# A gated linear-attention layer feeding a two-layer network: the values of a wide step multiplied behind the next step's scores and states, and a new plan for the front

## The chip, the cores and the metric

The kernel runs on one core of one Trainium2 chip. The metric is the time of one execution on the device in microseconds (us), lower is better. Times are medians of several executions; the profile shows one execution.

## The reference

For each of 4 batches and 8 heads a recurrence runs over 768 positions with head dimension 40. It keeps a 40x40 matrix `C` and a vector `n`, decayed by a forget gate and fed by an input gate (both stabilised by a running maximum `m`). The output is gated, and the gated rows of all heads (320 wide, 3072 tokens) go through two matrix products with a softplus between:

```python
C = f_stab * C + i_stab * einsum('bhd,bhe->bhde', v_t, k_t)
n = f_stab * n + i_stab * k_t
denom = maximum(abs(n . q_t), 1.0)
y_t = sigmoid(o_t) * (C q_t) / denom
out = softplus(y @ w_in) @ w_out        # 320 -> 2048 -> 320
```

## The kernel before, in words

**Tiling.** The 3072 tokens are cut into 24 chunks of 128 tokens (one batch, 128 positions); a *step* `s` computes the attention of one chunk, all 8 heads. Three steps make a *tile* of 384 tokens; there are 8 tiles `t`. For each tile and each of 16 column blocks `f` of the hidden layer, `products()` issues 8 matmuls 128x128 by 384 into a PSUM tile `hp` (line 931; operands are split in a high and a low part, hence 8), ScalarE takes softplus twice (lines 819, 820), VectorE forms the low part `gl` (line 823), and 9 matmuls 128x128 by 320 add into the three output tiles `po` (line 894). A block's 9 output matmuls come two blocks after its `hp`. So TensorE's stream is: 8 of `hp`, 9 of `po`, 8 of `hp`, and so on, 128 blocks in all.

**Steps.** Steps 0 to 5 are *plain*; they must be ready before or soon after the products begin. Steps 6 to 23 (tiles 2 to 7) are *wide*. A wide step has: `load`, `fb` (decays from DRAM), `scan` (line 403), `vw` and `vi` (values weighted for the states and for the outputs, line 417), `ga` = `scores` (line 444, 32 trace records of small matmuls), `st` = `states` (line 457, 32 records), `pm` (`by_decays`, line 465, VectorE reads the scores), `cp` (`keep_states`, ScalarE copies the states out), `old`, `mid`, `new` (the recurrent state on GpSimd), `gc` = `values_wide` (lines 606 and 618, 32 records each), `ym`, `ya` (lines 625, 629: VectorE reads the values), `yd`, `rd` (a round trip through DRAM that turns the layout), `fin`, `end`, `xh`, `xl` (normalise, gate, split; the slice of `X` that the tile's products read).

**What sets the order.** `products()` counts its own large matmuls, `n` = 17 a block. Each piece of other work is an event with a due value of `n`; `tick(n)` issues all events that are due behind the n-th large matmul, and each engine then runs its instructions in that order. Due values come from offsets in `wide_step` (line 804) relative to a `base` per step, and, for steps 0 to 8, for the weight conversions and for the gates, from the table `WHEN` (line 988). `PICK` (line 1038) names engines (V VectorE, A ScalarE, G GpSimd), `WARM` how many filler matmuls `keep_warm` (line 697) issues at each of 11 places in the front. `CHAIN` and `needed` (lines 735, 743) only assert that the order is legal.

**PSUM.** Of eight banks `ps_h` has three, one bank each (tag `hp`), `ps_a` one pair (tag `pa`), the outputs three. Before, a wide step's scores and states share the pair, and the same step's values take the pair some 20 `n` later:

```python
z.ga = pair(f"ga{z.n}", spare)                    # line 437
z.gc = gc = pair(f"gc{z.n}")                      # line 597
("ga", scores, 14), ("st", states, 14), ... ("gc", values_wide, 36),
```

Of the kernel before, what the change touches and what calls it, by code (L numbers as in the profile page):

```python
# [40 lines left out]
def mlstm_moe_kernel(  # L41
# [393 lines left out]
    def scores(z, spare=False):  # L435

        z.ga = pair(f"ga{z.n}", spare)
        for i in range(2):
            for q in range(NQ):
                ts = slice(q * Q, (q + 1) * Q)  # L440
                for y in range(2):
                    for x in range(2):
                        rows, g = slice(x * PP, x * PP + D), y * 2 + i
                        nc.tensor.matmul(  # L444
                            z.ga[y * Q : (y + 1) * Q, x, (i * NQ + q) * Q : (i * NQ + q + 1) * Q],
                            z.k[rows, g, ts], z.q[rows, g, ts], start=True, stop=True,
                        )
        z.qs = range(1 if z.last else NQ)

    def states(z):  # L450

        for q in z.qs:
            for i in range(2):
                for y in range(2):
                    for x in range(2):
                        j, w, c0 = (q * 2 + i) * 2 + x, D if x else PP, CP0 + (q * 2 + i) * E
                        nc.tensor.matmul(  # L457
                            z.ga[x * PP : x * PP + w, y, c0 : c0 + E],
# [4 lines left out]
    def by_decays(z):  # L463
        pw = z.pw.rearrange("p (x z) t -> p x (z t)", x=2)
        nc.vector.tensor_tensor(pw, z.ga[:, :, 0:CP0], pw, op=ALU.mult)  # L465
        z.pm = z.pw

    def keep_states(z):
        z.cp = p2.tile([PP + D, 2, NQ, 2, E], F32, tag="cp", bufs=4, name=f"cp{z.n}")
        w = len(z.qs) * 2 * E  # L470
        copy(
            pick(f"cp{z.id}", "A"),
            z.cp[:, :, 0 : len(z.qs)].rearrange("p y q z e -> p y (q z e)"), z.ga[0 : PP + D, :, CP0 : CP0 + w]
# [269 lines left out]
    def needed(kind, z):  # L743
        need = [(k, z.s) for k in CHAIN.get(kind, "").split()]
        if kind == "xh":
            need.append(("end" if z.wide else "xp", z.s))
        if kind in ("mid", "new", "gc") and z.c > 0:
# [43 lines left out]
    def plain_step(z, times):  # L791
# [3 lines left out]
            ga=lambda z: scores(z, z.s in SPARE_A), pm=by_decays, st=states, cp=keep_states, old=decay_old,  # L795
# [8 lines left out]
    def wide_step(z, base):  # L804
        d = 18 + 30 * (z.s == NH)
        for name, f, t in (
            ("fb", decays, -64), ("load", load, -48), ("vi", gate_values, -12), ("scan", decay, -8), ("vw", state_values, 2),
            ("old", decay_old, 6), ("fc", load_decays, 8), ("ga", scores, 14), ("st", states, 14), ("pm", by_decays, 19),
            ("cp", keep_states, 21), ("mid", mid_state, 24), ("new", new_state, 30), ("gc", values_wide, 36),
            ("ym", scale_wide, 42), ("ya", add_wide, 42), ("yd", write_wide, 45), ("rd", read_wide, 78),  # L810
            ("fin", finish_wide, 127 + d), ("end", end_wide, 128 + d), ("xh", high_wide, 131 + d), ("xl", low_wide, 134 + d),
# [173 lines left out]
    def finished(t):  # L985
        return all(s in ended for s in range(t * NG, (t + 1) * NG))

    WHEN = {'l0': -300, 'p0': -299, 'k0': -298, 'wl0': -297, 'p1': -296, 'j0': -295, 'load0': -294, 'w0_0_0': -293,
# [155 lines left out]
```

## Time and profile before

| | |
|---|---|
| median of 3 runs | 454.08 us (452.62 to 455.22) |
| the profiled execution | 449.44 us |
| its span, first to last instruction | 447.3 us |
| TensorE busy | 430.3 us (96%) |
| VectorE, ScalarE, GpSimd busy | 265.7, 212.2, 93.4 us |
| mean granted TensorE clock | 0.992 of full speed |

How to read it: a row of the timeline has a start, a duration and an instruction group with its count; successive matmuls overlap in the pipeline, so the pace is the distance between starts, not the duration. Records of small fp32 matmuls are twice the matmuls in the code.

### The profile page before, as it was taken

The page shows a single profiled execution, that of the slowest core. Times are in us where ns is not written, and L with a number is a line of the kernel's source. Part 1 is how long each engine was busy: PE and PEld are TensorE (multiplying, and loading weights), DVE is VectorE, ACT ScalarE, POOL GpSimd, SP SyncE. Part 2 cuts the span into 40 slices and gives each one's busy share as a digit, 9 for nine tenths or more (in the row PEclk, how much of TensorE's full clock was granted, in tenths as well). Part 3 has the DMA queues.
Part 4 walks back from the last instruction along what each step waited for, and adds up shares of the span by engine and source line. Part 5 has one row for each costly group of instructions (what it writes and reads, how often), then busy time and mean ns, then how long its engine had stood idle before and what let it go on. Part 6 is the DMA issues. An engine that isn't in the chain of part 4 may idle for free.

```text
span 447.3 us, 12745 instructions
## 1 busy us (share of the span) xinstructions
PE 430.3 (96%) x5312; PEld 410.7 (92%) x5312; DVE 265.7 (59%) x469; ACT 212.2 (47%) x458; POOL 93.4 (21%) x158
## 2 busy tenths in 40 slices
PE   6788899999999999999999999999999999999996
PEld 6668788998999999999999999999999999999996
DVE  5897999778878565456456465465465465322211
ACT  4678885668436323544236333453236333333332
POOL 1621343523222311311311311111211210000000
PEclk9969999999999999999999999999999999999999
DMA  7788597752654542643353443644443530001001
GB/s 200 217 252 256 159 246 194 252 150 93 165 129 147 164 135 78 164 118 105 113 146 88 128 122 86 168 92 121 123 119 107 135 92 24 20 1 44 1 0 45
DMA packets 52089, 55.93 MB, mean 125 GB/s; under 512 B 5664, under 2 KB 42176, under 8 KB 52032
## 3 DMA queue, kind: packets, MB, share of 16 engines
q1 hardware_dynamic: 49008, 51.68, 41.3%
q10 hardware_dynamic: 3024, 3.44, 2.2%
q8 instruction: 41, 0.67, 0.6%
q14 instruction: 16, 0.13, 0.1%
HBM read 46.47 MB, written 8.64 MB: 123 GB/s over the span
## 4 chain that ended last, share of the span: by engine, by line
PE 84%; DVE 6%; DMA 5%; ACT 2%; issue 1%; SPq 1%; ACTq 0%; DVEq 0%
PE hp L931 38%; PE po L894 37%; DMA wr<-in_w_in 3%; PE ga L444 3%; PE gc L606 2%; PE gc L618 2%; PE ga L457 2%; DMA qk<-in_qk 1%; DMA fz_d<-g 1%; DVE wil L296 1%; DVE sgi L258 1%; DVE wol L306 1%; DVE sgo L258 1%; DVE pw L465 1%; SPq L277 0%
## 5 line engine op out<-in xcount | busy, mean ns | idle before, releaser
L931 PE MATMUL hp<-X,wih 128*128 128x384 f32 x768 | 180.7, 340 | 0.0
L819 ACT ACTIVATE gh<-hp 128x384 fp32r<-128x384 f32 x128 | 62.9, 491 | 175.0 <-PE hp L931 160.4
L931 PEld LDWEIGHTS hp<-X,wih 128*128 128x128 f32 x768 | 132.7, 188 | 1.6 <-DVE X L685 0.3
L823 DVE TENSOR_TENSOR gl<-hp,gh 128x384 fp32r<-128x384 f32 x128 | 70.7, 555 | 99.1 <-ACT hp L820 98.9
L894 PE MATMUL po<-wol,gh 128*128 128x320 f32 x384 | 81.9, 312 | 0.0
L894 PE MATMUL po<-woh,gh 128*128 128x320 f32 x384 | 81.3, 311 | 0.0
L894 PE MATMUL po<-woh,gl 128*128 128x320 f32 x384 | 80.6, 310 | 0.7 <-DVE gl L823 0.7
L931 PE MATMUL hp<-X,wil 128*128 128x384 f32 x256 | 66.2, 338 | 0.0
L894 PEld LDWEIGHTS po<-woh,gh 128*128 128x128 f32 x384 | 65.1, 188 | 0.7 <-issue 0.3
L894 PEld LDWEIGHTS po<-woh,gl 128*128 128x128 f32 x384 | 62.3, 188 | 1.2 <-DVE gl L823 1.0
L894 PEld LDWEIGHTS po<-wol,gh 128*128 128x128 f32 x384 | 62.8, 188 | 0.6 <-issue 0.2
L820 ACT ACTIVATE hp<-hp 128x384 f32<-128x384 f32 x128 | 62.2, 486 | 0.0
L931 PEld LDWEIGHTS hp<-X,wil 128*128 128x128 f32 x256 | 46.2, 188 | 0.2
L417 POOL TENSOR_TENSOR vw<-vt,gw 128x328 f32<-128x328 f32 x21 | 16.2, 770 | 108.7 <-DVE gw L408 100.6
L403 DVE TENSOR_TENSOR_SCAN pw<-fb,ident 128x512 f32<-128x512 f32 x24 | 29.1, 1212 | 0.0
L465 DVE TENSOR_TENSOR pw<-ga,pw 128x512 f32<-128x512 f32 x23 | 15.8, 686 | 18.0 <-PE ga L457 17.6
L515 POOL TENSOR_TENSOR c<-c,cp 104x164 f32<-104x164 f32 x20 | 10.1, 506 | 75.7 <-ACT cp L728 70.0
L625 DVE TENSOR_TENSOR y<-gc,y 112x512 f32<-112x512 f32 x18 | 12.4, 691 | 19.0 <-PE gc L618 19.0
L444 PEld LDWEIGHTS ga<-qk 40*64 40x64 f32 x736 | 13.0, 134 | 6.6 <-issue 4.4
L728 ACT COPY cp<-ga 104x328 f32<-104x328 f32 (+1 forms) x22 | 9.2, 416 | 19.3 <-DVE pw L465 15.0
L417 POOL TENSOR_TENSOR values_in<-vt,gT 128x328 f32<-128x328 f32 x16 | 12.1, 756 | 28.2 <-PE gc L618 18.8
L444 PE MATMUL ga<-qk 40*64 40x64 f32 x736 | 16.3, 224 | 1.4 <-DMA qk<-in_qk 0.9
(153 smaller groups left out, 434.7 us busy)
## 6 DMA issues: line engine op xcount, KB each, us to landing
vt<-in_vk SPq DMA_DIRECT2D x24, 324.0 KB
qk<-in_qk SPq DMA_DIRECT2D x48, 160.0 KB
fb<-fz_d SPq DMA_DIRECT2D x42, 128.0 KB
wo<-in_w_out SPq DMA_DIRECT2D x8, 640.0 KB
wr<-in_w_in SPq DMA_DIRECT2D x8, 512.0 KB
eg<-in_oT SPq DMA_DIRECT2D x6, 576.0 KB
yd<-y SPq DMA_DIRECT2D x36, 96.0 KB
out<-ob ACTq DMA_DIRECT2D x21, 160.0 KB
```

Source lines behind the costliest of these rows:

```text
L403: nc.vector.tensor_tensor_scan(z.pw.rearrange(flat), z.fb.rearrange(flat), ident4.rearrange(flat), 0.0, ALU.mult, ALU.add)
L417: e.tensor_tensor(to, of, by.unsqueeze(3).broadcast_to([to.shape[0], a, b, w]), op=ALU.mult)
L444: nc.tensor.matmul(z.ga[y * Q : (y + 1) * Q, x, (i * NQ + q) * Q : (i * NQ + q + 1) * Q], z.k[rows, g, ts], z.q[rows, g, ts], start=True, ...
L465: nc.vector.tensor_tensor(pw, z.ga[:, :, 0:CP0], pw, op=ALU.mult)
L515: nc.gpsimd.tensor_tensor(heads(z.cm), heads(z.cm), z.cp[:, :, 0], op=ALU.add)
L625: nc.vector.tensor_tensor(y2, z.gc[0 : PP + EP, :, 0:CP0], y2, op=ALU.mult)
L728: (nc.scalar.copy if eng is nc.scalar else eng.tensor_copy)(to, of)
L819: nc.scalar.activation(gh, hp, AF.Softplus)
L820: nc.scalar.activation(hp, hp, AF.Softplus)
L823: nc.vector.tensor_tensor(gl, hp, gh, op=ALU.subtract)
L894: nc.tensor.matmul(po[j], a[:, j * 128 : (j + 1) * 128], w[:, f, :], start=(first and left[j] == 2), stop=(last and left[j] == 0),)
L931: nc.tensor.matmul(hp, a, r, start=(i == 0), stop=(i == len(seq) - 1))
```

## The change

For wide steps, `ga` and `st` become one event `group`. It takes the scores and states into two single banks of the tag `hp` (instead of the pair), and behind them, in the same event, issues `values_wide` of the step before, which alone keeps the pair: four banks in one stretch of small matmuls. So step s's values are multiplied with step s+1's scores and states; step 6's group has none behind it (step 5 is plain), and step 23's values stay an event of their own. `by_decays` and `keep_states` of a wide step become two instructions each, one for each bank. `vi` moves from 12 ahead of `base` to 20 behind it. Everything from `ym` on now hangs on `after`, the place of the next group; `fc` (line 342) moves too. For steps of tile 3 and later the spacing of groups is 85, 85 and 102 of `n`; each lies at n = 14 modulo 17, behind the seventh of nine output matmuls. The front's times, engines and fillers are set anew.

```diff
+    def group(z):
+        scores(z, [ps_h.tile([128, HG, L], F32, tag="hp", name=f"g{x}{z.n}").rearrange("p j t -> p (j t)") for x in "ab"])
+        states(z)
+        before = steps[z.s - 1]
+        if before.wide:
+            values_wide(before)
+            did.add(("gc", before.s))
+        did.add(("st", z.s))
...
-                            z.ga[y * Q : (y + 1) * Q, x, (i * NQ + q) * Q : (i * NQ + q + 1) * Q],
+                            z.ga[x][y * Q : (y + 1) * Q, (i * NQ + q) * Q : (i * NQ + q + 1) * Q],
...
-        nc.vector.tensor_tensor(pw, z.ga[:, :, 0:CP0], pw, op=ALU.mult)
         z.pm = z.pw
+        if z.wide:
+            for x in range(2):
+                nc.vector.tensor_tensor(pw[:, x], z.ga[x][:, 0:CP0], pw[:, x], op=ALU.mult)
+            return
+        nc.vector.tensor_tensor(pw, z.both[:, :, 0:CP0], pw, op=ALU.mult)
...
+        if z.wide:
+            for y in range(2):
+                copy(
+                    pick(f"c{'pq'[y]}{z.id}", "A"),
+                    z.cp[:, y, 0 : len(z.qs)].rearrange("p q z e -> p (q z e)"), z.ga[y][0 : PP + D, CP0 : CP0 + w],
+                )
+            return
...
+        if kind == "vi" and z.s > NH:
+            need.append(("gc", z.s - 1))
...
-    def wide_step(z, base):
+    def wide_step(z, base, after):
         d = 18 + 30 * (z.s == NH)
+        g = after - base
         for name, f, t in (
-            ("fb", decays, -64), ("load", load, -48), ("vi", gate_values, -12), ("scan", decay, -8), ("vw", state_values, 2),
-            ("old", decay_old, 6), ("fc", load_decays, 8), ("ga", scores, 14), ("st", states, 14), ("pm", by_decays, 19),
-            ("cp", keep_states, 21), ("mid", mid_state, 24), ("new", new_state, 30), ("gc", values_wide, 36),
-            ("ym", scale_wide, 42), ("ya", add_wide, 42), ("yd", write_wide, 45), ("rd", read_wide, 78),
-            ("fin", finish_wide, 127 + d), ("end", end_wide, 128 + d), ("xh", high_wide, 131 + d), ("xl", low_wide, 134 + d),
+            ("fb", decays, -64), ("load", load, -48), ("scan", decay, -8), ("vw", state_values, 2), ("old", decay_old, 6),
+            ("ga", group, 14), ("pm", by_decays, 17), ("cp", keep_states, 17), ("vi", gate_values, 20), ("mid", mid_state, 24),
+            ("new", new_state, 30), ("fc", load_decays, g - 34),
+        ) + ((("gc", values_wide, g),) if z.s == NS - 1 else ()) + (
+            ("ym", scale_wide, g + 5), ("ya", add_wide, g + 5), ("yd", write_wide, g + 8), ("rd", read_wide, g + 42),
+            ("fin", finish_wide, g + 91 + d), ("end", end_wide, g + 92 + d), ("xh", high_wide, g + 95 + d),
+            ("xl", low_wide, g + 98 + d),
         ):
...
-        LEAD, TS = 174, 16 * 17
-        EARLIER = 26
-        for s in range(NH, NS):
-            z = steps[s]
-            base = TS * z.t - LEAD - EARLIER - TS * (NG - 1 - z.g) // NG if z.t > WIDE else (183, 264, 344)[z.g]
-            wide_step(z, base)
+        TS = 16 * 17
+        at = [(190, 258, 326)[s - NH] if s < NH + NG else TS * (s // NG) - 272 - 85 * (NG - 1 - s % NG) for s in range(NH, NS)]
+        for s, base in enumerate(at, NH):
+            wide_step(steps[s], base, at[s - NH + 1] + 14 if s < NS - 1 else base + 46)
```

The tables are replaced whole. What the prediction speaks of, in the order in which the new `WHEN` issues it: the loads of steps 0 and 1 (`load0`, `load1`) now stand ahead of the first load of `w_in` (`wl0`), which stood ahead of both; the first conversions (`w0_0_0` and on) stand behind the first two steps' scores; `k10` comes behind the first block's eight matmuls.

```diff
-    WARM = {0: 6, 1: 5, 2: 0, 3: 3, 4: 0, 5: 1, 6: 0, 7: 3, 8: 0, 9: 5, 10: 4}
+    WARM = {0: 8, 1: 0, 2: 2, 3: 0, 4: 0, 5: 0, 6: 6, 7: 2, 8: 0, 9: 7, 10: 9}
```

In `PICK`, ahead of the first product, the two subtractions of line 195 leave VectorE for GpSimd (`gc0`, `gc1`), and the first low weights of line 296 (`wl0`) and one `vw` come to VectorE.

## Rows read from the trace of the kernel before

**Rows 1.** The page: engines' busy time, share of the span, instructions.

```profile
PE 430.3 (96%) x5312; PEld 410.7 (92%) x5312; DVE 265.7 (59%) x469; ACT 212.2 (47%) x458; POOL 93.4 (21%) x158
```

**Rows 2.** Busy time by stretch: before products, mixed front, mid, steady part.

```profile
core 0: us, PE busy (x) PEld busy (x) DVE busy (x) ACT busy (x) POOL busy (x), PEclk, DMA share, GB/s
0.00:33.20 33.20, 24.56 (x490) 20.34 (x490) 26.27 (x58) 19.78 (x42) 11.98 (x31) 0.90 0.77 225
33.20:75.00 41.80, 37.97 (x564) 33.63 (x557) 37.50 (x70) 35.14 (x84) 11.64 (x15) 1.00 0.76 214
75.00:140.00 65.00, 64.11 (x837) 61.52 (x836) 51.88 (x86) 38.52 (x83) 24.30 (x32) 1.00 0.57 163
140.00:443.60 303.60, 303.60 (x3433) 295.25 (x3431) 149.91 (x258) 118.37 (x251) 45.48 (x80) 1.00 0.34 93
```

**Rows 3.** TensorE's timeline in the steady part: one wide step's two excursions.

```profile
232.58 0.51 PE L931 MATMUL hp<-X,wih 128*128 128x384 f32 x2
233.02 0.69 PE L444 MATMUL ga<-qk 40*64 40x64 f32 x32
...
234.08 0.71 PE L894 MATMUL po<-woh,gh 128*128 128x320 f32 x3
234.63 0.60 PE L894 MATMUL po<-wol,gh 128*128 128x320 f32 x3
235.07 0.60 PE L894 MATMUL po<-woh,gl 128*128 128x320 f32 x3
...
237.33 0.46 PE L894 MATMUL po<-wol,gh 128*128 128x320 f32 x2
237.72 0.68 PE L606 MATMUL gc<-qk,c 40*64 40x64 f32 x32
...
238.80 0.41 PE L894 MATMUL po<-wol,gh 128*128 128x320 f32 x1
239.05 0.60 PE L894 MATMUL po<-woh,gl 128*128 128x320 f32 x3
```

**Rows 4.** TensorE's timeline in the front: scores followed at once by another step's values.

```profile
19.53 0.69 PE L444 MATMUL ga<-qk 40*64 40x64 f32 x32 [0.40 <-PE po L457]
20.06 0.44 PE L545 MATMUL po<-cp,qk 40*64 40x41 f32 x10
```

**Rows 5.** TensorE's timeline: the only idle time behind 75 us.

```profile
111.03 0.68 PE L606 MATMUL gc<-qk,c 40*64 40x64 f32 x32 [0.89 <-DVE pw L465]
```

**Rows 6.** Timeline of all engines, one block: from its last `hp` matmul to `gl`.

```profile
230.22 0.60 PE L894 MATMUL po<-woh,gh 128*128 128x320 f32 x3
...
230.48 0.49 ACT L819 ACTIVATE gh<-hp 128x384 fp32r<-128x384 f32 x1 [1.83 <-PE hp L931]
...
231.39 0.56 DVE L823 TENSOR_TENSOR gl<-hp,gh 128x384 fp32r<-128x384 f32 x1 [0.74 <-ACT hp L820]
```

**Rows 7.** Groups of instructions by line: mean ns of one behind the busy us.

```profile
L823 DVE TENSOR_TENSOR gl<-hp,gh 128x384 fp32r<-128x384 f32 x128 | 70.7, 555 | 99.1 <-ACT hp L820 98.9
...
L465 DVE TENSOR_TENSOR pw<-ga,pw 128x512 f32<-128x512 f32 x23 | 15.8, 686 | 18.0 <-PE ga L457 17.6 <-ACT cp L728 0.4
...
L728 ACT COPY cp<-ga 104x328 f32<-104x328 f32 (+1 forms) x22 | 9.2, 416 | 19.3 <-DVE pw L465 15.0 <-PE ga L457 4.3
```

**Rows 8.** Timelines of VectorE and TensorE: the last slice of `X`, then its tile.

```profile
192.60 0.56 DVE L667 TENSOR_TENSOR X<-eg,X 128x384 fp32r<-128x384 f32 x1
...
196.89 0.85 PE L931 MATMUL hp<-X,wih 128*128 128x384 f32 x4
```

**Rows 9.** The chain that ended last, first microseconds: the first two large loads.

```profile
1.65 4.16 DMA wr<-in_w_in
...
5.83 6.33 DMA qk<-in_qk
```

**Rows 10.** TensorE's timeline behind the first products: fillers, and a wait.

```profile
36.76 1.05 PE L697 MATMUL po<-ident 128*128 128x128 f32 x8
39.06 0.41 PE L133 MATMUL pg<-ident,gt 32*64 32x16 f32 x8 [1.24 <-ACT cp L728]
```

More of the change, by code (lines that the diff above doesn't have):

```diff
@@ L433, in state_values, with scores @@
         scaled(f"vw{z.id}", "G", z.vw, z.v1, z.gw)
-    def scores(z, spare=False):
-        z.ga = pair(f"ga{z.n}", spare)
+    def group(z):
[6 more added lines that the diff above has]
+        did.add(("st", z.s))
+    def scores(z, banks):
+        z.ga = banks
         for i in range(2):
@@ L448, in scores, with plain_scores @@
         z.qs = range(1 if z.last else NQ)
+    def plain_scores(z):
+        z.both = pair(f"ga{z.n}", z.s in SPARE_A)
+        scores(z, [z.both[:, x] for x in range(2)])
     def states(z):
@@ L457, in states @@
                         nc.tensor.matmul(
-                            z.ga[x * PP : x * PP + w, y, c0 : c0 + E],
+                            z.ga[y][x * PP : x * PP + w, c0 : c0 + E],
                             z.kt[y * Q : (y + 1) * Q, j * D : j * D + w], z.vw[y * Q : (y + 1) * Q, q, x * 2 + i],
@@ L470, in keep_states @@
         w = len(z.qs) * 2 * E
+        if z.wide:
[5 more added lines that the diff above has]
+            return
         copy(
             pick(f"cp{z.id}", "A"),
-            z.cp[:, :, 0 : len(z.qs)].rearrange("p y q z e -> p y (q z e)"), z.ga[0 : PP + D, :, CP0 : CP0 + w]
+            z.cp[:, :, 0 : len(z.qs)].rearrange("p y q z e -> p y (q z e)"), z.both[0 : PP + D, :, CP0 : CP0 + w]
         )
@@ L746, in needed @@
             need.append(("end" if z.wide else "xp", z.s))
+        if kind == "ga" and z.wide:
+            need.append(("vw", z.s))
+            if steps[z.s - 1].wide:
+                need += needed("gc", steps[z.s - 1])
+        if kind == "vi" and z.s > NH:
+            need.append(("gc", z.s - 1))
         if kind in ("mid", "new", "gc") and z.c > 0:
@@ L794, in plain_step @@
             load=load, fb=decays, scan=decay, vi=gate_values, vw=state_values, sig=out_gate,
-            ga=lambda z: scores(z, z.s in SPARE_A), pm=by_decays, st=states, cp=keep_states, old=decay_old,
+            ga=plain_scores, pm=by_decays, st=states, cp=keep_states, old=decay_old,
             mid=mid_state, new=new_state, gc=lambda z: values(z, z.s in SPARE_C), sum=sum_values, nrm=norm, sg=scale_gate, x=gated,
@@ L986, in finished @@
         return all(s in ended for s in range(t * NG, (t + 1) * NG))
-    WHEN = {'l0': -300, 'p0': -299, 'k0': -298, 'wl0': -297, 'p1': -296, 'j0': -295, 'load0': -294, 'w0_0_0': -293,
[48 rows of a table removed]
-    WARM = {0: 6, 1: 5, 2: 0, 3: 3, 4: 0, 5: 1, 6: 0, 7: 3, 8: 0, 9: 5, 10: 4}
-    PICK = {'vi0': 'A', 'wi00': 'G', 'ol0': 'V', 'wl2': 'V', 'ol1': 'V', 'ol2': 'V', 'wl4': 'V', 'oh6': 'V', 'wh7': 'V',
[6 rows of a table removed]
+    WHEN = {'l0': -300, 'p0': -299, 'k0': -298, 'p1': -297, 'l1': -296, 'p2': -295, 'p3': -294, 'j0': -293, 'load0': -292,
[47 rows of a table added]
+    WARM = {0: 8, 1: 0, 2: 2, 3: 0, 4: 0, 5: 0, 6: 6, 7: 2, 8: 0, 9: 7, 10: 9}
+    PICK = {'wi00': 'G', 'ol0': 'V', 'wl2': 'V', 'wl4': 'V', 'oh6': 'V', 'x2': 'V', 'wm10': 'V', 'wm30': 'V', 'wl6': 'V',
[7 rows of a table added]
     with in_order():
```

108 rows, old and new, of tables (PICK, WHEN) are left out of this document.

## The prediction, made before the changed kernel had run

> **What bounds the kernel now.** I read the page first. TensorE is busy for 430.3 of 447.3 us, the next engine for 265.7 [rows 1]. A share over the whole span mixes stages, so the second view is busy time by stretch [rows 2]. Before 33.2 us, where the products begin, TensorE is idle for 8.6 us and VectorE for 6.9. From 33.2 to 75 TensorE is idle for 3.8. From 75 to 140 it is idle for 0.89, in one place, where a step's values wait for VectorE's `pw` [rows 5]. From 140 to 443.6 it is never idle, and VectorE works half of the time (149.9 of 303.6). So behind 75 us the end is set by TensorE's own stream alone: only less TensorE time there, or an earlier start, can shorten the run.
>
> The third view is TensorE's timeline, read by the distance between starts. Three output matmuls take 0.44 us (234.63 to 235.07), 0.147 each [rows 3]. Two of them start at 237.33, so the next could start at 237.62; the values start at 237.72, 0.10 later. They leave at 238.80, and the one output matmul there is followed by the next at 239.05, 0.25 instead of 0.147: 0.10 more. The scores and states show the same: an `hp` matmul should take 384/320 of 0.147, 0.176, so two from 232.58 would end at 232.93, and the scores start at 233.02 (0.09); behind them three output matmuls take 0.55 instead of 0.44 (0.11). Each **excursion** from large to small matmuls thus costs 0.20 us beside its own work, 1.06 us for scores and states and 1.08 for values.
>
> **The change, part by part.** *Excursions.* Before, 18 wide steps make 36. After, 18 groups and the last step's separate values make 19: 17 fewer. The trace has no group of a wide step, so the price of the seam inside one, from states to values, is bounded from both sides. From above: it costs as much as an excursion, 0.20, and nothing is gained. From below: nothing, and 17 x 0.20 = 3.4 us go. The nearest row is one in the front where 32 records of scores, begun at 19.53, are followed by another step's values at 20.06 [rows 4]: 0.53 us for 32, as long as scores take in front of states with no seam. I take 3.4. The matmuls themselves are the same in number and size.
>
> *The stall at 111 us.* The values now come a step later than their `pm`, some 85 large matmuls or 13 us, so the wait of 0.89 us [rows 5] goes. What is late next is a bank, below.
>
> *Banks.* The group's two tiles take the `hp` banks of the two blocks before the current one. The block behind the group then takes the bank of the block just ahead of it, instead of one three blocks old. The group stands behind seven of nine output matmuls, so from the last `hp` matmul of block k to the first of block k+1 there are nine output matmuls (1.32) and the group (1.06 + 1.08 + 0.20), 3.66 us. The bank is free when `gl` is formed: in a plain block the output matmuls start at 230.22 and `gl` ends at 231.95, 1.73 us later [rows 6]. That leaves 1.9 us to spare; I take nothing for steps 9 to 23. If this cover goes, a stall of the missing part comes at every group. Step 6's group has no values in it (2.6 us of cover, in a stretch where VectorE is 80% busy, 51.88 of 65.0 [rows 2]), and steps 6 to 8 have fillers of conversions around them. Between nothing and one VectorE instruction in front in each of three groups (3 x 0.7, by the rows for `pw` [rows 7]) I take +0.4, as only one of the three has the short cover.
>
> *Split reads.* `gl` on 384 columns takes 555 ns and `pw` on 512 takes 686 [rows 7]: 1.02 ns a column, so two halves of 256 take about 0.42 each, 0.16 more than one. The two state copies cost at most one more copy, 0.42 [rows 7], of ScalarE a step. VectorE and ScalarE have 154 and 185 us free in the steady part [rows 2] and the next block needs these banks more than 2.7 us later: nothing. The bound is what they could add to the bank's wait, contained in the rival below.
>
> *Moved events.* `vi` waits on GpSimd for the values of the step before, in the group just ahead of it; behind it on GpSimd are `mid` and `new`, needed a step later: nothing, GpSimd is 15% busy there (45.48 of 303.6 [rows 2]). On SP's queue `fc` moves behind other loads but keeps its 34 matmuls ahead of `ym`; `yd` now stands right behind the `fb` loads of two steps on, and ahead of the next `load`; it waits for `ya`, and `load` is due 15 matmuls (2.4 us) later and is wanted 40 later still: nothing, and if `ya` were late, `load` would be late by that less 6 us. The tight one is the last step of a tile: its `xl` was due at 48 of `n` ahead of the tile's multiple and is now due at 40, 8 matmuls or 1.3 us later. Before, that slice was written by 193.16 and the tile's first matmul started at 196.89, 3.7 us later [rows 8]; 2.4 are left: nothing.
>
> *The front.* The same conversions and steps in another order. Its loads follow one another: the first `w_in` load ends the chain's first piece at 5.81, the first queries and keys then take until 12.16 [rows 9]. With the attention loads first, steps 0 and 1 can begin up to 4 us sooner and the weights come later, where they are wanted later too. The work is unchanged, so at best the idle time of VectorE before 33.2 (6.9) and of TensorE from there to 75 (3.8) goes: -10.7. At worst the order is as much worse; a bound is the same 8.6 us of TensorE's idle time once more. The fillers of `k10` grow from 4 to 9. Eight records of them take 1.05 us, ahead of a wait of 1.24 [rows 10], so five more would cost 1.3 if nothing waited there. As a whole I take -1.0, far from the ends, because VectorE works 26.3 of the first 33.2 us and 37.5 of the next 41.8 [rows 2], and an order cannot shorten work.
>
> **Sum:** -3.4 - 0.9 + 0.4 - 1.0 = -4.9 us on the profiled execution's 449.44 (447.3 of span and 2.1 around it): 444.5. The runs' median, 454.08, is 1.0% above that execution, so I scale: 454.08 x 444.5 / 449.44 = 449.1 us.
>
> **The rivals.** *Banks run short (no change).* If VectorE's queue delays `gl` of block k by more than 1.9 us, block k+1 waits at each group. A scan (1.2 us) and a tail of `fin` and `end` together would do it, since `gl` stands in line behind them. A wait of 0.2 us a group gives 17 x 0.2 = 3.4 back: 452.5. For it: three banks do the work of five. Against it: where the events lie, `gl` of block k is issued ahead of the group's own reads, and `fin` falls 7 or 24 matmuls behind a group, not ahead of one. The Trainium skill (Perfetto Trace Analysis, Optimization Strategy) says that the same gap repeating on the engine that should be saturated can mean there is too little PSUM for the next tile. By that rule this change would put such gaps where before there are none, and the trace so far shows none.
>
> *The seam costs as much as an excursion (no change).* Then the change doesn't do what it says; only the stall and the front remain, -1.5 us, 452.6. Against it: rows 4, though those values have another shape.
>
> *The front loses (slower).* The first `w_in` load is put behind two steps' loads. VectorE takes its queue in order: a conversion that waits for ScalarE, which waits for that load, holds the later steps' scores and the last slices of the first `X`, and with them the first product. Each us of delay at 33.2 is a us at the end, as nothing behind it is idle. It decides once it exceeds the 3.9 us gained elsewhere by 2.3, which is 6.2 us later, a first product near 39.4. Two loads of 4 to 6 us each [rows 9] bring that into reach. With 8 us lost: 449.44 - 3.9 + 8 = 453.5, scaled 458.2.
>
> *The front loses a little (no change):* 2 to 4 us, 451.9 to 454, from longer fillers or a conversion too late for the second or third weight pair.
>
> **How the numbers follow.** A measurement of this kernel can tell about 0.5% (2.3 us) from no change. Forecast 0.58, and inside it the front may gain up to 4 us more. Banks short 0.12, seam 0.05, front a little worse 0.12, front much worse 0.13. Of the forecast nearly all is below 451.8, of the next three most is within 0.5%: faster 0.60, same 0.26, slower 0.14. For 8 in 10 the range reaches from the forecast with 4.6 us more gained in the front (444.5) to just above no change (455.0); this leaves out the much worse front and a still better one.
>
> **What would show it.** TensorE's timeline behind 140 us: per wide step one excursion of 2.14 us with 0.10 on either side, no start late at states to values. An idle entry of `ga` or `hp` with the releaser `gl` would show the bank rival. In the busy time by stretch TensorE's idle time before the first product and from there to 75 us shows the front's part, as does the time of the first `hp`. The forecast is wrong if the span from step 9's group to the end has not fallen by about 14 x 0.20, or if the first product starts later than 36 us.

## The result and the profile after

The changed kernel's median is 441.19 us (439.56 to 442.37, 6 runs). The kernel before, run beside it, had 453.3 us (449.43 to 455.22, 6 runs): ratio 0.9755 [0.9712, 0.9798], estimated over all runs (the two medians alone give 0.9733), **faster by 2.5%**. Runs more than 1.5% above the quickest of their kernel are left out of every comparison here: three of twelve in one experiment, and one of the kernel before. The forecast of 449.1 had the direction; its range ended at 444.5, and the gain was larger. Profiled execution against profiled execution it is 440.25 against 449.44, 9.2 us less.

The page and the busy time by stretch of the changed kernel answer to [rows 1] and [rows 2]:

```profile
PE 426.7 (97%) x5326; PEld 413.4 (94%) x5326; DVE 263.9 (60%) x489; ACT 214.1 (49%) x487; POOL 97.6 (22%) x160
```

```profile
core 0: us, PE busy (x) PEld busy (x) DVE busy (x) ACT busy (x) POOL busy (x), PEclk, DMA share, GB/s
0.00:31.82 31.82, 24.47 (x494) 21.07 (x495) 25.03 (x58) 21.35 (x39) 12.04 (x31) 0.89 0.87 255
31.82:75.00 43.18, 42.17 (x587) 37.53 (x582) 39.47 (x75) 33.66 (x96) 13.27 (x20) 1.00 0.76 221
75.00:140.00 65.00, 65.00 (x907) 63.70 (x906) 53.24 (x96) 40.18 (x91) 27.44 (x37) 1.00 0.59 157
140.00:434.60 294.60, 294.60 (x3347) 290.90 (x3346) 145.67 (x262) 118.50 (x262) 44.88 (x74) 1.00 0.35 94
```

TensorE's idle time from the first product to 75 us is 1.0 instead of 3.8; the 0.89 of [rows 5] is gone, and behind 75 us there is none at all. What is saved behind 140 is therefore not waits, since neither kernel has one there: the same matmuls take less time.

TensorE's timeline of one group, to be held against the two excursions of [rows 3]:

```profile
231.58 0.31 PE L928 MATMUL po<-woh,gl 128*128 128x320 f32 x1
231.81 0.27 PE L454 MATMUL ga<-qk 40*64 40x64 f32 x1
...
232.62 0.20 PE L471 MATMUL gb<-vw,vt 64*40 64x41 f32 x1
232.65 0.23 PE L471 MATMUL ga<-vw,vt 64*64 64x41 f32 x1
232.66 0.23 PE L471 MATMUL gb<-vw,vt 64*64 64x41 f32 x1
232.66 0.26 PE L631 MATMUL gc<-qk,c 40*48 40x64 f32 x2
232.71 0.23 PE L471 MATMUL ga<-vw,vt 64*64 64x41 f32 x1
...
233.25 0.64 PE L643 MATMUL gc<-pw,values_in 64*48 64x64 f32 x30
233.83 0.56 PE L928 MATMUL po<-woh,gl 128*128 128x320 f32 x2
234.23 0.68 PE L965 MATMUL hp<-X,wih 128*128 128x384 f32 x3
```

The entry costs 0.09 (0.23 from the output matmul to the group, less its 0.147) and the exit 0.11 (0.40 for two, less 0.29), as forecast. Inside, from 231.81 to 233.83, the group takes **2.02 us**, not the 2.14 that 1.06 and 1.08 made. The reason stands at the seam: the values' first records start at 232.66, before the last two of the states, 0.85 behind the group's start. Before, 1.06 passed from the start of the scores to the start of the next large matmul, and 0.16 of it behind the start of the last record of the states (233.93 to 234.08). So a part of what I had read as the small matmuls' own work was the time until a *large* one followed, and that time is saved once per seam: by these rows 0.32 us a step, not 0.20.

For what follows I count `hp` matmuls as products, 8 a block; "product 128" is the start of the one with that number (0 the first), read from each trace. "Last" is the start of the last output matmul.

```
us from / to              first  0-64   64-128  128-384  384-768  768-last   128-last
before                    33.21  33.90  25.93   103.85   152.41   94.00      350.26
changed                   31.82  32.41  26.26   101.85   149.79   92.58      344.22
```

Before product 128 the changed kernel is 2.5 us ahead (90.50 against 93.04), behind it it gains another 6.0.

### The profile page after: what moved, and what is told of

Same layout as the page of the kernel before. It is cut to its first block, busy times and chain, and to the rows that moved or that the text cites. A ratio compares the mean times of both kernels' runs of the same rounds, so it can differ in the third digit from the quotient of the medians.

```text
span 438.3 us, 12822 instructions
## 1 busy us (share of the span) xinstructions
PE 426.7 (97%) x5326; PEld 413.4 (94%) x5326; DVE 263.9 (60%) x489; ACT 214.1 (49%) x487; POOL 97.6 (22%) x160
## 4 chain that ended last, share of the span: by engine, by line
PE 84%; DMA 8%; DVE 5%; issue 1%; SPq 1%; ACT 0%; POOL 0%; DVEq 0%; POOLq 0%
PE hp L965 38%; PE po L928 37%; DMA wr<-in_w_in 4%; DMA wo<-in_w_out 3%; PE ga L454 2%; PE gc L643 2%; PE gc L631 2%; PE ga L471 1%; DMA og<-in_o 1%; DVE sgi L256 1%; PE gb L454 0%; PE gb L471 0%; DVE gl L857 0%; DVE sgo L256 0%; SPq L373 0%
## 5 line engine op out<-in xcount | busy, mean ns | idle before, releaser
L965 PE MATMUL hp<-X,wih 128*128 128x384 f32 x768 | 176.3, 338 | 0.0
L965 PEld LDWEIGHTS hp<-X,wih 128*128 128x128 f32 x768 | 134.3, 188 | 0.4 <-DVE X L710 0.3
L928 PE MATMUL po<-woh,gl 128*128 128x320 f32 x384 | 83.3, 313 | 0.0
L417 POOL TENSOR_TENSOR vw<-vt,gw 128x328 f32<-128x328 f32 x19 | 14.0, 738 | 122.5 <-DVE gw L408 119.7
L403 DVE TENSOR_TENSOR_SCAN pw<-fb,ident 128x512 f32<-128x512 f32 x24 | 30.3, 1264 | 0.2
L417 POOL TENSOR_TENSOR values_in<-vt,gT 128x328 f32<-128x328 f32 x15 | 11.1, 739 | 58.7 <-PE gc L643 58.7
L676 DVE RECIPROCAL nm<-nm 128x128 f32<-128x128 f32 x18 | 17.2, 953 | 0.6
L753 ACT COPY cp<-ga 104x164 f32<-104x164 f32 (+2 forms) x21 | 6.7, 320 | 20.7 <-DVE pw L482 15.8
L540 POOL TENSOR_TENSOR c<-c,cp 104x164 f32<-104x164 f32 x20 | 13.5, 676 | 11.4 <-ACT cp L753 7.0
L471 PE MATMUL ga<-vw,vt 64*40 64x41 f32 (+1 forms) x416 | 14.1, 216 | 1.7 <-issue 1.4
```

What stands on the lines that cost most here:

```text
L403: nc.vector.tensor_tensor_scan(z.pw.rearrange(flat), z.fb.rearrange(flat), ident4.rearrange(flat), 0.0, ALU.mult, ALU.add)
L417: e.tensor_tensor(to, of, by.unsqueeze(3).broadcast_to([to.shape[0], a, b, w]), op=ALU.mult)
L471: nc.tensor.matmul(z.ga[y][x * PP : x * PP + w, c0 : c0 + E], z.kt[y * Q : (y + 1) * Q, j * D : j * D + w], z.vw[y * Q : (y + 1) * Q, q, x ...
L540: nc.gpsimd.tensor_tensor(heads(z.cm), heads(z.cm), z.cp[:, :, 0], op=ALU.add)
L676: nc.vector.reciprocal(nm, nm)
L928: nc.tensor.matmul(po[j], a[:, j * 128 : (j + 1) * 128], w[:, f, :], start=(first and left[j] == 2), stop=(last and left[j] == 0),)
```

## The experiments

Eleven experiments ran, two of them repeats without an edit, in three groups, each group on a chip of its own with the kernel before beside it: 450.68 us there (448.69 to 454.22, 23 runs), 450.80 (449.0 to 455.37, 16 runs) and 451.12 (449.38 to 453.77, 7 runs). The same table for all of them:

```
us from / to              first  0-64   64-128  128-384  384-768  768-last   128-last
before, again             33.51  34.91  25.83   103.85   152.41   94.00      350.26
changed, again            33.34  32.17  27.40   101.86   149.79   92.58      344.22
groups cut in two         31.93  32.51  26.73   103.47   152.71   92.90      349.08
groups cut in three       33.51  32.51  28.90   104.93   155.93   93.26      354.12
groups inside a block     32.74  32.48  26.50   103.63   151.03   92.64      347.30
new front, old steps      32.98  33.26  26.31   106.06   152.64   94.18      352.88
old front, new steps      32.39  35.38  26.61   109.13   149.59   92.37      351.08
old order ahead           33.86  34.80  27.58   101.73   149.59   92.37      343.68
w_in first                36.60  32.23  27.64   101.87   149.79   92.58      344.23
four fillers              32.18  32.91  26.87   102.65   149.79   92.58      345.02
step 5's values inside    32.53  32.42  44.34   101.87   149.79   92.58      344.24
```

**The new front alone.** The kernel before, with the changed kernel's entries of `WHEN`, `PICK` and `WARM` for all that is not a wide step; steps 6 to 8 keep their places. Of the tables only the fillers are short enough to show:

```diff
...
-    WARM = {0: 6, 1: 5, 2: 0, 3: 3, 4: 0, 5: 1, 6: 0, 7: 3, 8: 0, 9: 5, 10: 4}
+    WARM = {0: 8, 1: 0, 2: 2, 3: 0, 4: 0, 5: 0, 6: 6, 7: 2, 8: 0, 9: 7, 10: 9}
```

> The kernel before with the new front alone: all entries of the three tables that do not belong to the wide steps 6 to 8 are those of the change; the wide steps, their two excursions and the PSUM banks are those of before. Theory A (the front gives what the excursions do not): of the 9.0 us by which the profiled span fell, 17 excursions at the 0.32 us that the group's rows show saved (2.54 before, 2.22 after) make 5.4, the stall at 111 us 0.9, and 2.7 are left for the front; the medians fell by 12.1, so up to 5.8. Expected: 2.5 to 6 us faster than before, first large matmul near 31.8 us. Theory B (the front gives nothing, the wide steps carry all): within 1 us of before.

451.85 us (449.47 to 455.24), ratio 1.0024 [0.9997, 1.0051]. It reaches product 128 0.5 us sooner than the kernel before (92.55), then loses 2.2 between 128 and 384, where TensorE is idle for 2.4 of the 65 us from 75 to 140: new conversions among old steps. As a whole, nothing: theory A is excluded.

**The new steps with the old front:** the changed kernel with the kernel before's entries for all that is not a wide step (the diff above, the other way round).

> The changed kernel with the front of before: groups, banks and the places of the wide steps are those of the change; the other entries of the tables are those of before. Theory A: 6.3 us faster than before (5.4 + 0.9), first large matmul near 33.2 us, and so 2.5 to 6 us slower than the changed kernel. Theory B: as fast as the changed kernel, 11 us faster than before. If it is slower than either by more than 2 us, the two parts depend on each other.

454.17 us (451.11 to 456.97, nine runs), ratio 1.0095 [1.006, 1.013]; the profiled execution is the quickest, 451.11. From product 384 on it is as quick as the changed kernel (149.59, 92.37), and it still loses, because 128 to 384 takes 109.13. The waits of TensorE from 31 to 140 us, and the busy time from 75 to 140:

```profile
PE gb L454 <- DVE gl L857: 2.9, 2, 2.3
PE pg L133 <- ACT cp L753: 1.6, 1, 1.6
...
PE hp L965 <- DVE gl L857: 0.4, 1, 0.4
```

```profile
75.00:140.00 65.00, 61.61 (x747) 59.30 (x746) 48.33 (x85) 36.59 (x90) 22.70 (x29) 0.95 0.50 141
```

This is **the bank rival, come true in another schedule**: twice the group's second bank waits for the `gl` that still reads it, 2.9 us in all, and once a product does, 0.4; the granted clock of this stretch is 0.95, where it is 1.00 in the changed kernel. Here the groups paid only with the front that keeps VectorE out of their way. "Steps" and "front" are no independent terms of a sum.

**Groups cut in two.** For steps 9 to 23 the values stand two large matmuls behind the group: 15 more excursions.

```diff
-        if before.wide:
+        if before.wide and z.s < 9:
...
-        ) + ((("gc", values_wide, g),) if z.s == NS - 1 else ()) + (
+        ) + ((("gc", values_wide, g + 2 if z.s < NS - 1 else 37.5),) if z.s > 7 else ()) + (
```

> The changed kernel, but for steps 9 to 23 the values of the step before are issued two large matmuls behind the group instead of in it: 15 excursions more, nothing else moved. If an excursion costs the 0.20 us that was predicted: 15 x 0.20 = 3.0 us slower than the changed kernel. If it costs the 0.32 us by which a step's TensorE time fell: 4.8 us slower. If the saving came from elsewhere (the banks, the later values): within 1 us. The span from 140 us to the last output matmul shows it without the front.

447.32 us (445.6 to 449.09), ratio 0.9913 [0.9882, 0.9944]. From product 128 to the last it takes 349.08 instead of 344.22: 4.86 for 15 excursions, **0.32 each**. TensorE's timeline of one such step:

```profile
234.51 0.31 PE L928 MATMUL po<-woh,gl 128*128 128x320 f32 x1
...
235.81 0.56 PE L928 MATMUL po<-woh,gl 128*128 128x320 f32 x2
236.30 0.68 PE L631 MATMUL gc<-qk,c 40*64 40x64 f32 x32
236.80 0.65 PE L643 MATMUL gc<-pw,values_in 64*48 64x64 f32 x32
237.38 0.96 PE L965 MATMUL hp<-X,wih 128*128 128x384 f32 x4
```

The values take 1.08 again, from 236.30 to 237.38, as they did before the change.

**Groups cut in three:** scores, two large matmuls, states, two large matmuls, values, for steps 10 to 23; 29 more excursions than the changed kernel.

```diff
-        states(z)
+        if z.s < 10:
+            states(z)
...
+        ) + ((("st", states, 14),) if z.s > 9 else ()) + ((("gc", values_wide, g + 2 if z.s < NS - 1 else 37.5),) if z.s > 7 else ()) + (
```

> The changed kernel with the group of steps 10 to 23 cut in three: scores, two large matmuls, states, two large matmuls, the values of the step before. 29 more excursions than the changed kernel, 14 more than the kernel cut in two (span 443.8, 5.5 over the changed kernel for 15). Theory 'an excursion costs 0.30 to 0.32 us, because its small matmuls end in a tail that I had counted as their own work': 29 x 0.31 = 9.0 us over the changed kernel, a span of 447.3, twice the loss of the cut in two. Theory of the prediction, 0.20 each: 5.8 over, 444.1. Rival 'the cut in two lost its time by where the values stood, not by their number': scores and states apart cost little, since both read no bank that VectorE holds, and the span is 443.8 to 445. Per tile of 16 blocks (50.9 us in the cut in two, 49.93 in the changed kernel) the first theory gives 51.8 to 51.9.

450.88 us (449.39 to 454.93), ratio 1.0004 [0.9962, 1.0046]: the whole gain is gone. From 384 to 768, nine steps, 155.93 instead of 149.79: 6.14 for 18 excursions, 0.34 each. The second dose costs about what the first did (0.36 more for each further cut, against 0.32), and TensorE has no wait behind 75 us; so the seam from scores to states is worth about as much as that from states to values. 0.20 is excluded.

**Groups inside a block.** Steps 10 to 23 eight matmuls earlier, ahead of the last `hp` matmul of a block; meant to shorten the cover of the banks.

```diff
-        at = [... else TS * (s // NG) - 272 - 85 * (NG - 1 - s % NG) for s in range(NH, NS)]
+        at = [... else TS * (s // NG) - 272 - 85 * (NG - 1 - s % NG) - 8 * (s > 9) for s in range(NH, NS)]
```

> The changed kernel with the groups of steps 10 to 23 (and all that hangs on them) 8 large matmuls earlier, so that a group stands ahead of the last of a block's eight hp matmuls instead of behind seven of the nine output matmuls. From that block's last hp matmul to the next block, which takes the same bank, there are then only nine output matmuls, 1.32 us, where gl needs 1.73 us. Bank theory: TensorE waits at least 0.4 us for gl at each of 14 groups: 5.7 us or more slower than the changed kernel, with idle time before hp released by gl. Rival (the banks do not matter, three suffice wherever the group stands): within 1 us of it.

444.85 us (442.13 to 447.49), ratio 0.9859 [0.9822, 0.9895]. No idle time on a bank appears; a step costs 0.14 more (151.03 against 149.79 for nine). TensorE and ScalarE behind one such group:

```profile
237.10 0.60 PE L928 MATMUL po<-woh,gl 128*128 128x320 f32 x3
237.56 0.61 PE L965 MATMUL hp<-X,wih 128*128 128x384 f32 x2
```

```profile
236.80 0.49 ACT L854 ACTIVATE hp<-hp 128x384 f32<-128x384 f32 x1
237.21 0.30 ACT L753 COPY cp<-ga 104x164 f32<-104x164 f32 x1
237.40 0.30 ACT L753 COPY cp<-gb 104x164 f32<-104x164 f32 x1
```

Here the copies that free the group's banks stand behind both softplus of the block, and the first ends at 237.51, 0.05 before the next product. That product waits on ScalarE's semaphore, and starts while `gl` (237.42 to 237.97) still reads its own bank: in this program the block takes over a bank of the group and not the one of `gl`. As a squeeze on `gl` the experiment missed its aim, and says nothing for or against the bank rival. What makes the 0.14 was not traced further.

**The changed kernel, again.** No edit.

> The changed kernel once more, beside the others of this group and the kernel before on one chip. Two readings of its gain stand open: the profiled executions differ by 9.2 us (449.44 to 440.25), the medians by 12.1 (453.3 to 441.2). If the medians' gap is real, the ratio comes out near 0.9755 again and the kernel before near 453. If the first three runs of the kernel before were on its slow side, the kernel before comes out near 450.7, as in the group of experiments before, and the ratio near 0.979 to 0.980 (441.2 / 450.7). The first product: if its 31.8 us was the order's doing, it starts at 31.8 to 32 again; if runs scatter, anywhere up to 33.

442.96 us (441.94 to 446.55), ratio 0.9825 [0.9771, 0.988]; the difference of the medians is 7.8 us. Neither reading came out: the kernel before is near 450.8 as the second wants, but the ratio is nearer to 1 than either said: a gain of 1.8%, with 1.2 to 2.3% in its interval. Behind product 128 it takes the same 344.22 to the hundredth, but it gets there at 92.92 instead of 90.50: the first product starts at 33.34, and 64 to 128 takes 1.1 longer. The 1.1 is one wait, of TensorE for GpSimd's `x`: 1.46 us instead of 0.37. So these two runs of the same kernel differ by 2.4 us ahead of product 128 and not at all behind it.

**The kernel before, again.** No edit.

> The kernel before, profiled again. Its runs lie between 449.0 and 456, those of the changed kernel between 439.6 and 446.6, and its first profile (449.44) is one of its quickest. Open: what a run of 451 to 456 has that the profiled one has not. Theory 'the front scatters': from product 128 to the last output it takes 350.3 us again, within 0.4, and all that differs lies ahead of product 128 (93.0 us in the first profile; in four profiles with the new front 90.5, 91.2, 91.7 and 92.9). Theory 'the steady part scatters too', by a bank or by the clock: the 350.3 changes by over 1 us.

450.64 us, beside 451.12 (449.38 to 453.77). 350.26 behind product 128, to the hundredth the same; 94.25 ahead of it, 1.2 more than in the first profile. One stretch of its busy time differs:

```profile
50.00:60.00 10.00, 8.71 (x104) 7.78 (x103) 9.82 (x22) 8.18 (x27) 2.90 (x4) 0.84 0.61 188
```

There its clock is 0.84, and 1.00 in the same ten microseconds of the first profile, after the same idle share. No profile caught one of the runs of 453 to 456, so what those have stays open. Of the seven such runs beside the experiments four had a mean granted clock of 0.988 or 0.989, as all runs up to 449.6 had (0.988 to 0.992), so a lower clock alone is not it.

**The old order ahead of the first product,** with its fillers there; all behind it as in the changed kernel, and the engines too.

```diff
-    WHEN = {'l0': -300, 'p0': -299, 'k0': -298, 'p1': -297, 'l1': -296, 'p2': -295, 'p3': -294, 'j0': -293, 'load0': -292,
+    WHEN = {'l0': -300.0, 'p0': -299.03361344537814, 'k0': -298.06722689075633, 'p1': -296.1344537815126, 'l1':
...
-    WARM = {0: 8, 1: 0, 2: 2, 3: 0, 4: 0, 5: 0, 6: 6, 7: 2, 8: 0, 9: 7, 10: 9}
+    WARM = {0: 6, 1: 5, 2: 0, 3: 3, 4: 0, 5: 1, 6: 0, 7: 3, 8: 0, 9: 5, 10: 9}
```

> The changed kernel, but what is issued ahead of the first product stands in the order of the kernel before (the first w_in load again ahead of the attention loads) with its fillers there; all behind the first product is as in the changed kernel. Theory A 'the attention loads first is what the front gains by': the first product starts 1 us or more later than in the changed kernel of this group, product 64 at 66 to 67 instead of 64.2, and the time is 1.5 to 2.5 us longer, 442.7 to 443.7. Theory B 'the front gains behind the first product, by where conversions, steps 3 to 5 and the gates stand': the first product moves by less than 0.6 us, and the time by less than 0.8. A price above 3 us would be a third case: a conversion that came too late in the old order for the new places behind it.

446.49 us (443.28 to 448.82), ratio 0.9892 [0.9835, 0.9949]; 3.5 us over the changed kernel of its group. The first product comes at 33.86, 0.5 later; the larger loss lies just behind it, 2.6 up to product 64:

```profile
40.52 0.41 PE L133 MATMUL pg<-ident,gt 32*64 32x16 f32 x8 [1.14 <-DVE pw L484]
```

```profile
40.00:50.00 10.00, 9.48 (x103) 8.77 (x105) 9.01 (x20) 8.39 (x22) 2.75 (x4) 0.83 0.85 242
```

A wait of 1.14 us ahead of the gates, and ten microseconds at a clock of 0.83, so part of them at the lower of its two levels (1.2 and 2.4 GHz): 1.14 and, as an estimate, 10 x 0.17 are 2.8, about the 2.6 lost there. Neither theory fits: the first product moved by less than theory A wants, the time by more than 3 us.

**`w_in` first.** One event of the changed kernel is moved: the first `w_in` load goes ahead of the attention loads.

```diff
-        'j4': -282, 'l2': -281, 'fb0': -280, 'wl0': -279, 'fb1': -278, 'k2': -277, 'scan0': -276, 'p6': -275, 'p7':
+        'j4': -282, 'l2': -281, 'fb0': -280, 'wl0': -297.5, 'fb1': -278, 'k2': -277, 'scan0': -276, 'p6': -275, 'p7':
```

> The changed kernel with one event moved: the first w_in load is issued behind the first queries and keys' place in the old order, ahead of the two steps' loads, on SP's queue. The order of the conversions stays. Theory 'the order of the loads sets the first product': it starts 1 us or more later (the attention loads are 4 to 6 us each), above 33.5, and the time is 1 to 2 us over the changed kernel's 442.96 on this chip. Theory 'VectorE's work sets it, not the loads' (it was busy 24.2 of the first 31 us): the first product stays between 31.8 and 33.3 and the time within 1 us.

445.42 us (443.99 to 446.22), ratio 0.986 [0.9809, 0.991]; the changed kernel had 0.9825 and 442.96 in its group. The first product starts at **36.60** instead of 33.34 (the changed kernel's later profile), and the last output matmul at 440.70 instead of 437.14, 3.56 later: what is lost at the first product is lost at the end. By the medians it is 3.5 us behind the kernel with four fillers, below, which ran beside it. Its chain that ended last shows the load that comes late:

```profile
3.36 4.14 DMA gt<-in_gates
7.52 6.89 DMA qk<-in_qk
16.89 5.67 DMA og<-in_o
```

The first queries and keys land at 14.41, against 12.16 in the kernel before [rows 9], and the load of the output gates at 22.56, against 15.72 in the changed kernel (there it stands on the chain from 11.74 for 3.98). Among the new order of conversions, the order of the loads is a term by itself. It is not so among the old one: there `w_in` stands first too, and the first product starts at 32.39 to 33.86 in four profiles.

**Four fillers** instead of nine at the last place.

```diff
-    WARM = {0: 8, 1: 0, 2: 2, 3: 0, 4: 0, 5: 0, 6: 6, 7: 2, 8: 0, 9: 7, 10: 9}
+    WARM = {0: 8, 1: 0, 2: 2, 3: 0, 4: 0, 5: 0, 6: 6, 7: 2, 8: 0, 9: 7, 10: 4}
```

> The changed kernel with 4 fillers instead of 9 at its last place, ahead of the first gates. 9 fillers take 2.27 us there (18 records). By the prediction's term they cost nothing where TensorE would wait anyway: a wait of about 1.2 us for ScalarE or VectorE appears ahead of the gates, as in the kernel before, and the time stays within 1 us. Rival, by the granted clock: the kernel with the old order ahead had such a wait of 1.14 us there and a granted clock of 0.83 in the 10 us behind it, while in the changed kernel, without the wait, it is 1.00; then the wait costs up to 10 x (1 - 0.83) = 1.7 us more, some 445. Third: the fillers themselves are in the way, and it is 1 us faster.

441.96 us (441.21 to 444.13), ratio 0.9794 [0.9731, 0.9856]: no difference that these runs can show.

```profile
34.39 1.16 PE L722 MATMUL po<-ident 128*128 128x128 f32 x8
35.30 0.94 PE L965 MATMUL hp<-X,wih 128*128 128x384 f32 x4
36.08 0.51 PE L965 MATMUL hp<-X,wil 128*128 128x384 f32 x2
36.54 0.41 PE L133 MATMUL pg<-ident,gt 32*64 32x16 f32 x8
```

No wait takes the place of the fillers; my reason was wrong. Product 16 comes 6.2 us behind the first instead of 7.3, and by product 64 the 1.1 us are gone again, in part in a wait for `X` (0.9 instead of 0.4); behind 64 it waits 0.9 for `x`. What TensorE saves at that place does not last.

**Step 5's values inside the first group,** their reads and slices of `X` 85 matmuls later; one excursion fewer.

```diff
-        125.667, 'gc5': 126.5, 'sum5': 129.5, 'nrm5': 130.333, 'w5_0_0': 130.667, 'j12': 131.333, 'sg5': 131.667, 'f7':
...
+        'load7': -134.5, 'w3_1_5': 125.333, 'w4_1_0': 125.667, 'gc5': 211.6, 'sum5': 214.6, 'nrm5': 215.433, 'w5_0_0':
+        130.667, 'j12': 131.333, 'sg5': 216.767, 'f7': 138.333, 'w4_1_1': 138.667, 'w4_1_2': 139.5, 'x5': 227.6, 'f9': 145.5,
...
```

> The changed kernel with the values of step 5, the last plain step, issued right behind the first group (step 6), and their reads, normalisation and slices of X 85 matmuls later: one excursion fewer. By 0.31 an excursion the time falls by 0.3 us, which medians can hardly show (440.9 against 441.2); the trace should show the first group with 32 + 32 + 32 records and no separate values near 126 of n. Rival: step 5's chain on VectorE now falls together with that of step 6, ahead of the third tile's first products, and a wait for X appears at the tile's start: 1 us or more is lost.

459.12 us (458.61 to 463.72), ratio 1.0198 [1.0134, 1.0262]. The edit was my mistake: tile 1's products begin behind the tenth block, at product 80, and `products()` issues all that is queued until the tile's slices are written. The first group was drawn forward with them, from 82.7 us in the changed kernel to 71.9, where its weighted values `vw` were not ready:

```profile
80.15 0.33 PE L471 MATMUL ga<-vw,vt 64*64 64x41 f32 x2 [7.55 <-POOL vw L417]
...
88.98 0.69 PE L698 MATMUL xp<-ident,x 128*128 128x128 f32 x2 [6.04 <-DVE gw L408]
```

It shows what a group placed too early costs, and that such a stall is not made up: 16.9 us lost from product 64 to 128 (44.34 against 27.40), and the rest as in the changed kernel.

## Why the prediction was wrong in size

Between the two profiles: 444.5 was forecast for the changed one (before scaling), 440.25 came, 4.25 us less. Behind product 128 the forecast was 3.9 (17 excursions, the stall, less the banks) and 6.04 came; ahead of it 1.0 and 2.54; the rest, 0.6, lies behind the last output matmul and around the span, which the prediction had put at nothing. On top of that stands the scaling to the runs' median, the largest piece. Two steps failed, then: the price of an excursion and the scaling; they come first and last in this list.

- **Excursions: the price was mis-sized.** The step that failed is "0.20 us beside its own work, 1.06 us for scores and states and 1.08 for values". The entry and exit are right (0.09 and 0.11), but 1.06 and 1.08 were measured up to the next *large* matmul's start and so held another 0.12 of the excursion. It costs 0.30 to 0.34. Behind product 128 lie 35 excursions before and 18 after; 6.04 less 0.89 for the stall is 5.15 for 17 of them, 0.30 each. Cut in two it is 0.32, cut in three 0.34. I took the lower bound, nothing for the seam; the truth lay below that bound, since the seam also saves what I had put into the work. The Trainium skill (TensorEngine Tiling (Array Packing), Key Properties) says that a change of tiling mode drains TensorE. A loss of time between large and small matmuls, and records that overlap between states and values, agree with that; that the loss is such a drain no run here shows.
- **The stall at 111 us** is gone, as forecast, and nothing is late in its place; but what made the room is not the values' move. The stall was at step 7's values, which stood 13.05 us behind their scores (97.98 to 111.03) already before, and stand 14.41 behind them now (95.28 to 109.69). What moved is VectorE's `pw` of that step, 12.2 us behind the scores before and 1.6 now, by its new place in the table:

```profile
110.21 0.68 DVE L465 TENSOR_TENSOR pw<-ga,pw 128x512 f32<-128x512 f32 x1
```

```profile
96.86 0.42 DVE L482 TENSOR_TENSOR pw<-ga,pw 128x256 f32<-128x256 f32 x1
```

- **Banks: right in the steady part.** VectorE's timeline shows `gl` of the block ahead of the group, and the group's own reads:

```profile
231.80 0.56 DVE L857 TENSOR_TENSOR gl<-hp,gh 128x384 fp32r<-128x384 f32 x1 [2.10 <-ACT hp L854]
232.99 0.42 DVE L482 TENSOR_TENSOR pw<-ga,pw 128x256 f32<-128x256 f32 x1 [0.63 <-PE gb L471]
233.33 0.41 DVE L482 TENSOR_TENSOR pw<-gb,pw 128x256 f32<-128x256 f32 x1
```

  The bank is free at 232.36, the next product starts at 234.23: 1.87 us to spare, forecast 1.9. The +0.4 for steps 6 to 8 did not come. The rival is real all the same, as the kernel with the old front shows. The Trainium skill's rule that I weighed against this change (Perfetto Trace Analysis, Optimization Strategy), by which a repeating gap can mean too little PSUM, finds three gaps there (2.3, 0.7 and 0.4 us) and none in the changed kernel.
- **Split reads: right.** `pw` in two halves takes 0.42 and 0.41 us, forecast 0.42 each; the copies 0.28 each (mean of 13 and 13 behind 140 us), and TensorE waits for neither.
- **The front: right in kind, its size not well known.** I took -1.0. In six profiles with the whole new front ahead of product 128 (changed, again, cut in two, cut in three, inside a block, four fillers) product 128 comes at 92.2 in the mean, but anywhere from 90.5 to 94.9; in the two of the kernel before at 93.6: **-1.4**. Of it 0.8 is the first product (32.6 against 33.4), 1.9 lies from 0 to 64, where waits of 3.2 us in the first profile became 0.6, and 1.2 is given back up to 128. The latest, cut in three, had a wait of 1.83 for `x` and a granted clock of 0.91 from 75 to 95 us; without it the mean gain is 2.0. My reason, the attention loads first, is not shown. The kernel with `w_in` first shows that the new order of conversions needs them first; but with the old order ahead of the products, `w_in` first, the first product starts at 32.39 to 33.86, and with the new one at 31.82 to 33.51. The rival "the front loses" had the price right (each us at the first product is a us at the end: 3.3 and 3.56) and the sign wrong. The fillers' 1.3 is no cost either: five fewer changed nothing at the end that the runs can show.
- **The level: the scaling failed.** The step is "The runs' median, 454.08, is 1.0% above that execution, so I scale". The changed kernel's median lies only 0.2% above its profiled execution (441.19 and 440.25), and in the three later groups the kernel before is at 450.7 to 451.1, 0.3 to 0.4% above its first profile. On the chip of the repeat the measured parts, 1.4 ahead of product 128, 6.0 behind it and 0.6 at the ends, make 8.0 where the medians differ by 7.8; that they agree so well is luck, by the scatter of the first part. In the first comparison the kernel before was at 453.3 and the changed one at 441.2, 4 us more than the parts give. Those runs of the kernel before have no profile but the one at 449.44, and the cause stays open. With three runs shown, from 452.6 to 455.2, and a profiled one at 449.44, below all three, the range should have reached down by that difference of 4.6 us.

From 449.1 to the profiled 440.25 it is then 8.9 us: 4.6 of level (449.1 less 444.5), 2.1 of excursions and banks, 1.5 of the front in that run, 0.6 at the ends. The median of the changed kernel's runs lies 0.9 above that execution.

## What to carry to other kernels

Price a change of the stream by the distance from the last matmul of one kind to the first of the *next* kind, on both kinds of neighbour: "own work" measured up to a costly exit contains part of the exit. Where TensorE was never idle, moving small matmuls together gained as taking work away would, here 0.3 us per excursion, and putting them apart again cost the same. Check at which place of the schedule a gain can last: what was saved behind product 128 stayed, what was lost at the first product stayed lost, and what was saved between product 8 and 16 did not last. Set a forecast against a median of more than three runs, or against the profiled execution itself.

## What the runs showed that I had not expected

- The stretch from product 128 to the last output matmul repeated to the hundredth: 350.26 twice and 344.22 twice, while the time ahead of it moved by 1.2 and by 2.4 us. For one and the same program a part timed by such marks can be told far closer than medians tell it, which scatter by 2 us. Between programs with the same groups but other fronts or fillers it moved more, from 343.68 to 345.02, so the 4.86 us for 15 excursions are good to some tenths.
- The clock: the granted clock was below 1.00 in some stretches during or just behind a wait of TensorE in the front (0.83 with the 1.14 us in the old order; 0.66 from 40 to 50 us behind the 1.56 with the old front; 0.84 from 75 to 140 us with the waits of 7.55 and 6.04 us), and 1.00 from 31.82 us on in the changed kernel, whose longest wait there is 0.4. But it was 1.00 from 40 to 50 us in the kernel before, behind a wait of 1.24, and from 75 to 140 us in the old order, with one of 1.76. And 0.84 came in the kernel before, from 50 to 60 us, in a run whose idle time there equals that of a run at 1.00. What decides it these runs do not show.
